# One more row group of an output projection with plain products in place of a seven-product scheme, and a new fixed order of all tasks

## The chip, the core and the metric

The kernel runs on one core of one Trainium2 chip. The metric is the device time of one execution in microseconds (us), the median over runs. The engines are named as in the profile: PE is the matrix engine (PEld its weight loads), DVE the vector engine, ACT the scalar engine, POOL the GpSimd engine, and SP the engine whose queue issues most of the transfers. Each engine works through its own instructions in the order in which the program lists them.

## The reference

Attention over 4 batches, 8 heads, 768 positions of 64 elements, followed by a gated feed-forward block over the 3072 resulting rows:

```python
scores = (q @ k^T) / 8                       # per batch and head
keep   = causal                              # heads 0, 2, 6
keep   = causal & (key < 4 | q - key < 64)   # the other heads
x      = softmax(where(keep, scores, -1e9)) @ v      # -> (3072, 512)
g      = x @ w_gate                          # (512, 1536)
out    = (g * sigmoid(g) * (x @ w_val)) @ w_out      # (1536, 512), float32
```

## The kernel before

**Tiles and groups.** Queries come in 24 tiles of 128 rows, loaded in pairs. Loads land in eleven raw buffers. A tile goes through casts (`cq`, `ck`, `cx`), transposes on PE (`trq`, `trk`) with copies out of PSUM (`evq`, `evk`), scores on PE (`sc`), exponentials on ACT (`ex`), multiplications by a 0/1 mask on DVE or POOL (`mask`, L577), value products on PE (`val`), a normalisation on DVE (`nm`), a transpose back (`xtr`) and a copy (`xe`). Four tiles make a group, so there are six groups of 512 rows. For each group, twelve column blocks of the hidden layer are made: `gate` and `vals` are four 512-column matmuls each (L732; in group 0 some are split in two halves of 256), followed by `tanh` on ACT (L738) and two DVE operations, `stt1` (L742) and `stt2` (L748), that leave the block in `h_sb`, which holds two groups at a time.

**The output projection** of a group multiplies 512 rows of hidden activations by `w_out`. It exists in two forms.

- *Plain*: for each of the four row tiles, twelve 512-column matmuls accumulate in one PSUM bank (`outproj`, L766), then one copy (`oevac`) and one 256 KB store. In terms of 2 by 2 blocks this is eight block products. Group 5 uses it.
- *Seven products*: the hidden block and `w_out` are cut into 2 by 2 blocks, and seven products of sums of blocks replace the eight (`seventh`, L812, twelve 256-column matmuls each). It needs sums of hidden blocks (`hsum`, eight per group, L799, on DVE or POOL), sums of weight blocks once for all groups (`wsum`, twelve, L412, kept in `wt_sb`), and eight gathering steps per group (`gathered`, seven additions on DVE at L828 and one copy), then two 512 KB stores. Groups 0 to 4 use it (`SEVENS = 5`).

**The order.** No scheduler decides at build time. Every step is a task of a `Plan`. Three strings, the work of an offline planner, fix everything: `ORDER` lists the tasks (and a few filler matmuls on an identity, `warm`) in the order in which they are issued, `WAYS` picks for each task which of its allowed engines runs it, and `SLOTS` picks its buffer or PSUM bank. A task issued earlier stands ahead of later ones in its engine's queue, and waits there for what it depends on.

Of the kernel before, what the change touches and what calls it, by code (L numbers as in the profile page):

```python
# [13 lines left out]


ORDER = (
    "000402061U1V071W03xx1c1d1e0920211Xy21f0C01050A22yG28292A231g1h1i1j1r1s1p1q1w081Z1b1axh2B2CzG2E2D"
    "2F2N2O2L2M2W2c2d2e0B2426252G2H2I0D2X2f1Y1k1l1m1t1u1v2g2i2h2j2l2m1n2J1o1y1z2K272P2Q2R0g0y98999A1x"
    "2t30312x382y0F3C3I3J3K0h139c9S9T9d9U0m109B9C0n140G2o2p33349e0z9I2S2U2V9D9G9h9a9E9F9H9i9j2n9V9W0E"
    "2Y2a2Z9X9Y9Z9f9g9b9J9K3D3L2b2k2q2r2s2u3M3N3O3P3U3V329k9l0i169r9m9s9t2z9n9o3R3S353637399N9O119L9M"  # L20
    "9P9Q9R0H3F3H3E3b3l3m3i3j0l1FALAGAMANAH3W3X3f0o179u9v9pAI9q3T3G0q1D3Q3Y3Z3a3g3c0k1CA6ABA7A83kA9AA"
    "ACAD2T0j3n3o0t19A19wA23h3p3q2v3r3A3B2w3d3e0r1GAJAKA3AOAP3s3t0J3v439x9y0I3u4041420p1AA4A50K3y3x3z"
    "Ax0U15AEAFATAV4446454748494H4A4BB40wAuAvAwAy9zA00P5J0M4b0u18ASB5B6BEBFBGBdBeBf0s12B7B84L4M4NB9BA"
    "BBBYBZBgBhBaBC1E1M3w0V4O4P4W4CBbBc4DAUBDAzB0B14j4k4l0RBiBjBk0x1H1Q1R1T1S4E4F4GBHBIBlBm0vB2B31B1K"
    "1I1J1LAY1N1P0L4a4g4h4i5R0N4d4f4e4cAQAXARAZAW4p4qBTBUBVBOBPBQ4m4z4R4S5S5TApAqAr0bBWBX1OAe0O5I0Y7E"
    "4n4oBJBKBL0S0e4Q5O5P5Q4I0W6X6YAcAdAfAiAj4r56574J4KAaAbAgAhAkAo4T4U4V4X53AsAt5p5v5w54554u4v4s4t5f"
    "BMBN4w5g4x4y505c5l5dBRBSBpBrBnBo5B5C595A58AlAm4Y4Z515D5E5F5xBv0T5s5t520a5q5y5z60BqBsBuByC5Bt6465"
    "0cAnBw616C625G5HC10Z7H66D5D6D7CCCDCECoD8D90Q5L5K5NClCmCnCp7mCRCSCTCgChCi5h6J6KBzC07M7N7O5rCjCk0X"
    "7D5M5e5i5j5k5mC36VC2C4C6C7CB7I6W6L5U5V5W6G6H6ID0D1D2CvCwCFCGCxCe5X5Y5ZCMCNCyCzCO7lD3D467685u7k6M"
    "6N6e6f6gCUCV6b6c6d63696A6B6DCPCQCqCrCs5a5n5b5o7q7r7s6O6P6Q6SCbCcCdCf7J7K6E6FCWCXCYBxC8C9CA7L6R6h"  # L30
    "6i6j6k6l6uCtCu6T6UCKCZCaDDDFCHCICJENEOEPCLDCDE6mEDEEEFDtDuDv7t7u7v0f8T6n6o6p6qEIEJ0d8QDADGDBDH7o"
    "7X7Y7Z7a7g7b7cDwDxEKELEMEGEH6r6s6v6tDIDLDJ8U74757172737P7Q7RDeDfDgDyDzE0EQERDZDaDb7z807G76DhDiES"
    "ETEUE1E2EVEW6aDMDN7F7d777e7f7S7T7U8RDm6y6z707w7xDcDd6w6x7i7V7W7j7pE3E4E5DODPDj6Z78797AE881DkDlDn"
    "8W8X8Y7B7CDoDpDqEB7nFBFCFD878H8I8B8CE9DQDR7yE6E7EA8E8MEC8283FLFMFNFEFFDrDs7h848588868ZFOFPFn8D8F"
    "8G8a8b8c8k8l8f8g8h8d8e8VFGFHFIFaFbFcF6F7F8FiFVFWDKF9FAFXDSEZDUEaDTEbFkFlFJFKFmDYFfFgDVDWFoFhFj8J"
    "8K8N8LEXEYEdFpFqFrFsFtFQFRFS8p91928w8xFdFe8i8j8tFTEcElEe8S8m8n8o8q8uEfEi8vF1F2EjF3En8z90EwExEhFU"
    "Es8y9394DXEkEmEgEo898r8A958s8OF49697EpEqErEtEz8PGxHCHDGnFxFzEyH2GyF5GbGzGqEvGoEuF0GpGrGiGjH0H5Gk"
    "GvH3H1H4H6GsGtGuGwFYFZGlGYGZGaGcGJGKGLFuFvFwFyG0G2G4GdGeGfGmH7H8H9GRGgGhGOGPGTHEGUG1G6G7G5GFHAG3"
    "GCHBGVGWGXGAGQGSHFHGGMGNG8G9GDGGGHHHGBGEGIHIHJHMHNHKHLHOHRHPHQHSHTHWHXHYHbHUHVHZHaHcHd"
)  # L40
WAYS = (
    "000010000000000000000000000000000000000000000000000000000000222202022222202002220010101010101212"
    "020000000000000000000000110001212222011011000000100000001000220011011000001001000001001001001000"
    "000001220111011000001001000000010000010010000000002201120000000000010000000010010010000011000200"
    "200010010010010000000210100100000000000020102000001100000001001001000010002221101000000100100000"
    "020000100100000120120000201100000000100000002200001001000000000220112000000001000000010010001101"
    "201110001001000001000001101001001000001201102020000000001000000000010010000010000000000000000000"
    "000000000000000000000000000000000000000000000000000000000000000000000000100000000100000000000000"
    "000000000000000000000000000000000000000000000000000000000000001001000100000000000000000000000000"
    "000000000000000000000000000000000000000000000000001111110011000000000000000000000000000000000000"  # L50
    "000000000000000000000000000000000000000111110000100000000000100000000000000000000000000000000000"
    "000000000000000000000000000111110100110000000000000000000000000000000000000000000000000000000000"
    "00000000000000000000000010000000000010"
)
SLOTS = (
    "0015246374927435A772A445A6315997824058A38A501609221819001016041002241222230063601254461440016340"
    "656011214224222121043652064614232261606014354644521622063602461221046162644040343654462621302145"
    "600160216141211426361623606445601310362216320614025604224614041421402642562542516163424201406465"
    "604133263222541412634461606200005010410210124411031120024500140040110012330130002110011155022233"
    "031050200011002221015001401011100100401441250120510120130251113012411115121401501220005100430000"  # L60
    "013110000200100345500000202121500000211114301100125115412010041125124052131203005501111211023311"
    "1112131134100412210200023310531201144125302011050100012411241100410131043120200002102"
)
DIGITS = "0123456789ABCDEFGHIJKLMNOPQRSTUVWXYZabcdefghijklmnopqrstuvwxyz"

# [54 lines left out]
def kernel(  # L120
# [50 lines left out]
    P = Plan(RINGS)  # L171
# [49 lines left out]
    NK, HM = NJ // 2, DM // 2  # L221
    SEVENS = 5
# [193 lines left out]
    for i in range(3):  # L416
        for x in range(1, 5):
# [3 lines left out]
                                 deps=[T_w["o", i][0], T_w["o", i + 3][0]] + before))  # L421
# [412 lines left out]
        eng.dma_start(out=out[r0:r0 + 256, :].rearrange("(s p) n -> p s n", s=2),  # L834
                      in_=out_sb[:, x])

    T_hs, T_ga, T_p, T_stored = {}, {}, {}, {}

    def tasks_of_sevens(g, T_h):
        wo = [T_w["o", j][0] for j in range(6)]  # L840
# [55 lines left out]
    for g in range(NG):  # L896
# [3 lines left out]
        for j in range(NJ):  # L900
            parts = [(0, 256), (256, 512)] if g == 0 and j < HALVES else [(0, w)]
            for c in parts:
                a = P.add(f"gate{g}.{j}.{c[0]}", ["PE"],
                          (lambda g=g, j=j, c=c: gate(g, j, c, wg_sb, gs)),
                          deps=xs[c[0] // 128:c[1] // 128] + [T_w["g", j // 2][j % 2]],
                          takes=["gv"])
                th = P.add(f"tanh{g}.{j}.{c[0]}", ["ACT"],
                           (lambda g=g, j=j, c=c: tanh(g, j, c)), deps=[a], takes=["sig"])
                s1 = P.add(f"stt1 {g}.{j}.{c[0]}", ["DVE"],
                           (lambda g=g, j=j, c=c: stt1(g, j, c)), deps=[th], takes=["sil"])  # L910
                v_ = P.add(f"vals{g}.{j}.{c[0]}", ["PE"],
                           (lambda g=g, j=j, c=c: gate(g, j, c, wv_sb, vs)),
                           deps=xs[c[0] // 128:c[1] // 128] + [T_w["v", j // 2][j % 2]],
                           takes=["gv"])
                was = [T_p[g - 2, p] for p in ((6, 7) if j < NK else (3, 4))] if g > 1 else []
                s2 = P.add(f"stt2 {g}.{j}.{c[0]}", ["DVE"],
                           (lambda g=g, j=j, c=c: stt2(g, j, c)), deps=[s1, v_] + was)
                T_h.setdefault(j, []).append(s2)
                P.uses(a, "gv", s1)
                P.uses(v_, "gv", s2)  # L920
                P.uses(th, "sig", s1)
                P.uses(s1, "sil", s2)
                P.uses(T_first_x[g], "xt", a, v_)
        if g < SEVENS:
            tasks_of_sevens(g, T_h)
            continue
        last = None
        for tt in range(SIZES[g]):
            stores = []
            for x, (ring, lo, hi) in enumerate(pieces(g, tt)):  # L930
                for third in range(3) if x == 0 else [0]:
                    js = slice(third * 4, third * 4 + 4) if x == 0 else slice(0, NJ)
                    last = P.add(
                        f"out{g}.{tt}.{3 * x + third}", ["PE"],
                        (lambda g=g, tt=tt, x=x, js=js: outproj(g, tt, x, js)),
                        deps=[y for j in range(js.start, js.stop) for y in T_h[j]]
                        + [T_w["o", j // 2][0] for j in range(js.start, js.stop, 2)],
                        takes=[] if third else [ring], after=[last])
                    if third == 0:
                        head = last  # L940
                oe = T_oe[g, tt, x] = P.add(
                    f"oe{g}.{tt}.{x}", ["ACT", "DVE"], (lambda g=g, tt=tt, x=x: oevac(g, tt, x)),
                    deps=[last] + T_stored[g - 1, tt // 2], after=stores[:1])
                P.uses(head, ring, oe)
                st = T_st[g, tt, x] = P.add(f"st{g}.{tt}.{x}", ["SP", "ACT"], (lambda g=g, tt=tt, x=x: store(g, tt, x)),
                           deps=[oe])
                stores.append(st)
            for y in stores:
                P.lands(y)


    for number in P.order():
# [40 lines left out]
```

## Time and profile before

| what | value |
|---|---|
| median of 3 runs | 259.12 us (258.81 to 259.85) |
| the profiled execution, its own time | 258.92 us |
| its span in the profile | 256.9 us |
| granted PE clock | 1.0 |
| PE busy | 246.9 us (96% of the span) |
| DVE busy | 195.2 us (76%) |
| ACT busy | 154.8 us (60%) |
| POOL busy | 154.7 us (60%) |
| moved by transfers | 34.98 MB |

The profiled execution's own time is 2.0 us above its span, and the median is 0.2 us above the profiled execution. Busy time on PE is a modelled figure, since matmuls overlap. The spacing of their starts, which the chain of waits shows (for instance 64 matmuls in 13.81 us), tells what they cost when nothing holds them.

### The profile page before, as it was taken

The page shows a single profiled execution, that of the slowest core. Times are in us where ns is not written, and L with a number is a line of the kernel's source. Part 1 is how long each engine was busy: PE and PEld are TensorE (multiplying, and loading weights), DVE is VectorE, ACT ScalarE, POOL GpSimd, SP SyncE. Part 2 cuts the span into 40 slices and gives each one's busy share as a digit, 9 for nine tenths or more (in the row PEclk, how much of TensorE's full clock was granted, in tenths as well). Part 3 has the DMA queues.
Part 4 walks back from the last instruction along what each step waited for, and adds up shares of the span by engine and source line. Part 5 has one row for each costly group of instructions (what it writes and reads, how often), then busy time and mean ns, then how long its engine had stood idle before and what let it go on. Part 6 is the DMA issues. An engine that isn't in the chain of part 4 may idle for free.

```text
span 256.9 us, 5969 instructions
## 1 busy us (share of the span) xinstructions
PE 246.9 (96%) x2368; PEld 153.8 (60%) x2368; DVE 195.2 (76%) x337; ACT 154.8 (60%) x245; POOL 154.7 (60%) x161
## 2 busy tenths in 40 slices
PE   7989899998989999999999999999999999999995
PEld 3667755643565868665675656665565874466643
DVE  1569799998999789699997859578487778776740
ACT  5799987486948775765787785765736242231011
POOL 6489999926990968659705998506876505084000
PEclk9999999999999999999999999999999999999999
DMA  7999999998860067802007000000021003000043
GB/s 189 348 357 344 331 356 357 376 387 271 276 186 0 0 189 225 245 4 82 3 3 243 2 3 0 3 1 4 1 94 72 3 0 144 22 0 3 0 184 143
DMA packets 32331, 34.98 MB, mean 136 GB/s; under 512 B 1456, under 2 KB 22192, under 8 KB 32304
## 3 DMA queue, kind: packets, MB, share of 16 engines
q1 hardware_dynamic: 31888, 33.82, 41.0%
q10 hardware_dynamic: 416, 0.79, 0.8%
q8 instruction: 18, 0.29, 0.5%
q14 instruction: 9, 0.07, 0.1%
HBM read 28.31 MB, written 6.29 MB: 135 GB/s over the span
## 4 chain that ended last, share of the span: by engine, by line
PE 65%; POOL 11%; DVE 9%; DMA 6%; SPq 5%; issue 3%; POOLq 0%; DVEq 0%
PE banks L732 33%; PE banks L812 16%; POOL e L577 7%; PE banks L560 4%; PE banks L766 4%; SPq L349 4%; DMA raw<-in_moe_w_val_dram 3%; PE banks L587 3%; DMA raw<-in_moe_w_out_dram 2%; DVE h_sb L748 2%; DVE wt_sb L412 2%; PE banks L466 2%; PE banks L606 1%; POOL wg_sb L208 1%; POOL wv_sb L208 1%
## 5 line engine op out<-in xcount | busy, mean ns | idle before, releaser
L732 PE MATMUL banks<-xt,wg_sb 128*128 128x512 f16 (+1 forms) x304 | 71.2, 368 | 3.1 <-DVE sil L742 1.7
L732 PE MATMUL banks<-xt,wv_sb 128*128 128x512 f16 (+1 forms) x304 | 70.8, 368 | 0.0
L569 ACT ACTIVATE e<-banks 128x1024 f16<-128x1024 f32 (+2 forms) x68 | 59.0, 912 | 16.7 <-PE banks L560 8.8
L738 ACT ACTIVATE sig<-banks 128x512 f32<-128x512 f32 (+1 forms) x76 | 42.9, 577 | 41.9 <-PE banks L732 36.3
L577 POOL TENSOR_TENSOR e<-e,m 128x640 f16<-128x640 f16 (+1 forms) x31 | 54.8, 1783 | 19.8 <-ACT e L569 19.3
L742 DVE SCALAR_TENSOR_TENSOR sil<-sig,banks 128x512 f32<-128x512 f32 (+1 forms) x76 | 49.3, 656 | 18.5 <-ACT sig L738 15.7
L748 DVE SCALAR_TENSOR_TENSOR h_sb<-sil,banks 128x512 f16<-128x512 f32 (+1 forms) x76 | 49.1, 655 | 7.8 <-PE banks L732 6.0
L732 PEld LDWEIGHTS <-wg_sb 128*128 128x128 f16 x304 | 28.0, 97 | 31.7 <-issue 4.7
L732 PEld LDWEIGHTS <-wv_sb 128*128 128x128 f16 x304 | 28.4, 98 | 27.8 <-issue 0.2
L812 PEld LDWEIGHTS <-h_sb 128*128 128x128 f16 x360 | 34.5, 98 | 7.4
L799 POOL TENSOR_TENSOR hs_sb<-h_sb 128x768 f16<-128x768 f16 x8 | 13.3, 1668 | 27.9 <-DVE h_sb L748 21.0
L828 DVE TENSOR_TENSOR out_sb<-banks,out_sb 128x512 f32<-128x512 f32 x35 | 23.3, 686 | 5.5 <-PE banks L812 4.9
L799 POOL TENSOR_TENSOR h_sb<-h_sb 128x768 f16<-128x768 f16 x13 | 21.4, 1642 | 6.2 <-PE banks L812 5.0
L560 PE MATMUL banks<-qT,kT 64*128 64x128 f16 x472 | 21.6, 218 | 0.5 <-DVE xb L595 0.3
L812 PE MATMUL banks<-wt_sb,h_sb 128*128 128x256 f16 x180 | 22.0, 273 | 0.0
L812 PE MATMUL banks<-wo_sb,h_sb 128*128 128x256 f16 x180 | 21.9, 273 | 0.0
L560 PEld LDWEIGHTS <-kT 64*128 64x128 f16 x472 | 14.6, 94 | 11.6 <-issue 10.1
L587 PEld LDWEIGHTS <-e 128*128 128x128 f16 x472 | 16.9, 97 | 2.8 <-issue 0.5
L208 POOL CAST hq<-raw 128x1024 f16<-128x1024 f32 (+1 forms) x16 | 16.1, 1014 | 4.0 <-DMA raw<-in_k_dram 2.9
L587 PE MATMUL banks<-vt,e 128*128 128x65 f16 x472 | 17.9, 193 | 0.4 <-POOL vt L208 0.4
L595 DVE TENSOR_TENSOR xb<-banks,rc 128x512 f16<-128x512 f32 x24 | 16.6, 691 | 1.0
L466 PE MATMUL banks<-ident,hq 128*128 128x128 f16 x192 | 14.6, 219 | 1.7 <-DVE h_sb L748 1.0
(58 smaller groups left out, 249.0 us busy)
## 6 DMA issues: line engine op xcount, KB each, us to landing
raw<-in_v_dram SPq DMA_DIRECT2D x12, 512.0 KB, 6.2
raw<-in_q_dram SPq DMA_DIRECT2D x22, 256.0 KB, 5.2
raw<-in_k_dram SPq DMA_DIRECT2D x22, 256.0 KB, 5.9
out_dram<-out_sb SPq DMA_DIRECT2D x9, 512.0 KB, 2.9
raw<-in_moe_w_gate_dram SPq DMA_DIRECT2D x6, 512.0 KB, 8.2
raw<-in_moe_w_val_dram SPq DMA_DIRECT2D x6, 512.0 KB, 8.4
raw<-in_moe_w_out_dram SPq DMA_DIRECT2D x6, 512.0 KB, 7.4
raw<-in_q_dram SPq DMA_DIRECT2D x1, 512.0 KB, 4.4
```

The source lines that it names most:

```text
L208: ENG[task.way].tensor_copy(out=dst, in_=src)
L560: nc.tensor.matmul(sc[:, c:c + n, :], weights, moving, start=first, stop=last)
L569: nc.scalar.activation(out=to, in_=src, func=AF.Exp, scale=scale)
L577: ENG[task().way].tensor_tensor(out=ev, in0=ev, in1=mm, op=ALU.mult)
L587: nc.tensor.matmul(avs[t][:, odd, n * 66:n * 66 + 65], ee, vv, start=(m == 0), stop=(m == len(bl) - 1))
L732: nc.tensor.matmul(ps, wsb[:, kk, j * 128:(j + 1) * 128], xt[:, kk, c[0]:c[1]], start=(kk == 0), stop=(kk == 3))
L738: nc.scalar.activation(out=sg[g, j, c], in_=gs[g, j, c], func=AF.Tanh, scale=0.5)
L742: nc.vector.scalar_tensor_tensor(out=sl[g, j, c], in0=sg.pop((g, j, c)), scalar=1.0, op0=ALU.add, in1=gs.pop((g, j, c)), op1=ALU.mult)
L748: nc.vector.scalar_tensor_tensor(out=hs[g, j][:, c[0]:c[1]], in0=sl.pop((g, j, c)), scalar=0.5, op0=ALU.mult, in1=vs.pop((g, j, c)), op1=A ...
L799: ENG[T_hs[g, x][part].way].tensor_tensor(out=to, in0=a, in1=b, op=op)
L812: nc.tensor.matmul(rooms[g, p][:, x], left[:, j, 128 * x:128 * x + 128], right[:, j], start=(j == 0), stop=(j == NK - 1))
L828: nc.vector.tensor_tensor(out=cell(*to), in0=rooms[g, p], in1=cell(*other), op=ALU.add)
```

## The change

Group 0 goes over to the plain form. Groups 1 to 4 keep seven products, group 5 stays plain. The eight block sums of group 0 and its eight gathering steps are no longer there, and the twelve weight sums are first read by group 1. The dependencies follow: `stt2` of group 2, which overwrites the buffer of group 0, now waits for the plain products of group 0, and the gathering of group 1 waits for the landing of group 0's four stores.

The three strings are replaced as a whole, so every engine's queue is in another order. Some tasks change engine.

| tasks | before | after |
|---|---|---|
| filler matmuls besides the first ten | 14 | 13 |
| masks | POOL 31, DVE 7 | POOL 23, DVE 15 |
| hidden block sums | POOL 26, DVE 14 | POOL 23, DVE 9 |
| weight block sums | POOL 5, DVE 7 | POOL 6, DVE 6 |
| weight casts | POOL 15, ACT 5 | POOL 14, ACT 3, DVE 3 |
| gathering additions | DVE 35 | DVE 28 |
| block products (12 matmuls of 256) | 35 | 28 |
| plain matmuls of 512 or less | 60 | 108 |
| stores | 15 | 17 |

```diff
 ORDER = ( ...
-    "000402061U1V071W03xx1c1d1e0920211Xy21f0C01050A22yG28292A231g1h1i1j1r1s1p1q1w081Z1b1axh2B2CzG2E2D"
...
+    "0306021U1Vxz1c000105071W1Xy01f1g1h0A221dzI1i1j1e1p1q1r1w232B2C041s0920212829zG2E2F2A0C2W2c2d2D2L"
...
-    T_hs, T_ga, T_p, T_stored = {}, {}, {}, {}
+    T_hs, T_ga, T_p, T_stored, T_plain = {}, {}, {}, {}, {}
...
-                was = [T_p[g - 2, p] for p in ((6, 7) if j < NK else (3, 4))] if g > 1 else []
+                was = [T_p[g - 2, p] for p in ((6, 7) if j < NK else (3, 4))] if g > 2 else (
+                    T_plain[0] if g == 2 else [])
...
-        if g < SEVENS:
+        if 0 < g < SEVENS:
             tasks_of_sevens(g, T_h)
             continue
...
-                    deps=[last] + T_stored[g - 1, tt // 2], after=stores[:1])
+                    deps=[last] + T_stored.get((g - 1, tt // 2), []), after=stores[:1])
...
-            for y in stores:
-                P.lands(y)
+            T_stored.setdefault((g, tt // 2), []).extend(P.lands(y) for y in stores)
+            T_plain.setdefault(g, []).append(last)
```

More of the change, by code (lines that the diff above doesn't have):

```diff
@@ L16 @@
 ORDER = (
-    "000402061U1V071W03xx1c1d1e0920211Xy21f0C01050A22yG28292A231g1h1i1j1r1s1p1q1w081Z1b1axh2B2CzG2E2D"
[L18 to L36, printed above, removed]
@@ L37 @@
-    "Es8y9394DXEkEmEgEo898r8A958s8OF49697EpEqErEtEz8PGxHCHDGnFxFzEyH2GyF5GbGzGqEvGoEuF0GpGrGiGjH0H5Gk"
-    "GvH3H1H4H6GsGtGuGwFYFZGlGYGZGaGcGJGKGLFuFvFwFyG0G2G4GdGeGfGmH7H8H9GRGgGhGOGPGTHEGUG1G6G7G5GFHAG3"
-    "GCHBGVGWGXGAGQGSHFHGGMGNG8G9GDGGGHHHGBGEGIHIHJHMHNHKHLHOHRHPHQHSHTHWHXHYHbHUHVHZHaHcHd"
+    "0306021U1Vxz1c000105071W1Xy01f1g1h0A221dzI1i1j1e1p1q1r1w232B2C041s0920212829zG2E2F2A0C2W2c2d2D2L"
+    "2M2N2O0B25242G2H272e2I0D2X2f081b1Y1Z1k1l1m1a1t1u1x1v2g2h2i2l2j2k2t2m2o2p0m101n1y1z1o303133262P2Q"
@@ new lines @@
+    "2R342J2K0h139c9d9S9e9T9U0g0y98999A9B0F3C3I3J3K2n2U2V9G9D9E9h9i322S2x2y389C9j0n149k9l9f9g9F9H0z9N"
+    "9I9O9P0E2Z2Y2q2b2r2s2u119Q9R9J9K9X9Y9Z0G3D3L9L9M0i162a9V9W9a9b0l1F2z3M3N3R3S3O3P3b3T3W3X9r9s9tAG"
+    "AHAI3f9m9n9o35363g37390o179p9q9u9v3Q0k0H3E3F3HALAMAN0q3l3m3U3V1CA6A71DA90j19A8AA3n3i3Y3Z3o3a3j3c"
+    "9w9x3h0rA1A2A31GAJAK3G2v3d3e2wAE0I0J3v9y3p0p1A3u4041423A0w3k3q3r434445ABAC1E3s3tA4A5ADAFAOAP0s3B"
+    "BdBeBgBbBfBhBTBUBVBYBZBaBc49120v46474H2TB4B5B64A0u4BApAq1B4L4M4N9zA0Ar0x1HAsAtAkAlAm4C4D0Q5M0V0K"
@@ new lines @@
+    "3y3w3x3z4O4P4W0M4bB9BAB7B8BBBEBF18BCBDBG4j4k4lBWBXAzB0B10L4a4g4h4iAuAv484E4F4GAn0t15AQ1M1OAR1I1J"
+    "1L4QB2B3Aw0N4c4d0P5J4p4q4r4m4n4z0O5I0T5s5r0W6Y4IASATAVAWAU0d0UAo4R4S565758BOBPBQ5NAXAaAYAZ4T4U4V"
+    "4X1K1N1PAbAc6W0f4J4K4u4vAd4e4o4s4t0R5R5S5TAxAy1Q1R1T4Y4Z595A53BlAe5p5O5PBJBKBL4w4x544y55AfAgAhAi"
+    "5B0S0bBn4f6a5Q5c5d5f5gBMBN5v5w5xBHBI5L5qBiBp1S6X5051525CBRBSBkBmBo5h0c6V5y5zAjBj5D5E5F8UBqBsBr60"
+    "5GBy5l6465666162638V5t5HCMCND0D1CjD3CbD2CcD4C7CPCOC8C9CQCACBCqCdCrCsCgChCiCk5eBuBvBwBxBz5K5i5j5m"
@@ new lines @@
+    "5k6C6G7mBt0Y7E7M7N7OCe0X7D6H6ICHCICJ6M6NCf5U5V0eC0C2C16ZClCmCn6J6K6R676b6c6dCKCLCU5W5X5Y685ZCvCw"
+    "Cx7J7K5a5n5b5o696A6D6BCyCzCRCSCTCV6L0a7k7q7r6e6f6g5u6O6P6QCWCXCY6SCtCuCZ6T6U0Z7G7I7LCaD87p6k6l6m"
+    "7sC3C4C56E6F6h6u6i6j7P7Q7RCoCpDUDVDWENEOEPEQER6n6o6p6q7oCCCDCE7lEDEEEF7n6r6s6t6v74757172738QDXDY"
+    "EIEJEKDc7X7Y7Z7a7g7b7cC6CFCGD7D9DoDpDqDZDaDrDsDbDdD5D6DBELEMDADC7HEGEH7t7u7vE8E9EADtDuDv8283DDDG"
+    "DEDFEBEC7F7S7d7e7f7T7U7z8081DHDI6y6z7076777wDJDK6w7i6x7V7W7j787x7y798W8X8YDh7ADeDfDgDiDLDM7h8485"
@@ new lines @@
+    "8886878B8CE17B7CDyDzE0E2E6E3E4E5E78R8Z8a8E8F8G8H8I8DDjDkDlDQFGFHFIDNEUDODRDPDSDT8M8c8d8eFaFbDwDx"
+    "FcDmDnEVEXFLFMFNFJFKFOFPFBFCFDF1F2F3F4F5FVFWFXF6F78k8l8b8f8g8hF9FEFFF8FAEwExEy8J8K8N8LFfFgEWFkFl"
+    "FdFeFhFYFZFm8p91928w8x8yESETEYFnFo8T8i8j8t8zEaEbEcEk8S8m8u8v8n8q908oErEsEtEZEuEvFiFjFQFRFS939489"
+    "8r958O8P8AEzFTFUEeEfEi9697EgEhEjEmElEdEnEoEp8sGsGxGyGdGeGbGzGvGEGtGuGwGiGqEqGfGHGjGFFsFuF0GGFpFq"
+    "GIGnGoGlGMFwGkGmGTGWFrGpGYGUGZGrGVGXH5GOGJGKGaFxGcG0GRGLG7FyHAGPGNGQGSH7H8H9HBH0H1G5H2H3H4H6GgGh"
@@ L40 @@
+    "FtG3FvFzG1G2G4G8GAGBGCG6G9GDHCHDHEHFHGHHHIHJHKHLHMHNHOHPHRHSHQHTHWHUHVHXHY"
 )
 WAYS = (
[L42 to L50, printed above, removed]
@@ L51 @@
-    "000000000000000000000000000000000000000111110000100000000000100000000000000000000000000000000000"
-    "000000000000000000000000000111110100110000000000000000000000000000000000000000000000000000000000"
-    "00000000000000000000000010000000000010"
+    "000001000000000000000000000000000000000000000000000000000000221222222201012222200110111000101112"
+    "220101100000000000000000210022022222011001000000000000000100222220001000000001000000200000000000"
+    "002201220201000000001000000000010010010010000000002001100100010010010000022000010000000010002202"
@@ new lines @@
+    "100100000000000000000120000000100000000020001000000000100000001001000210122221201100000100100000"
+    "220100100100000220002011100000000100100000001201000001000000001200200000001001000000000000002100"
+    "221111001001000001000002101000001000002100120002010000000001000000021010000010000000000000000000"
+    "000000000000000000000000000000000000000000000000000000000000000000000000010000010001000010000000"
+    "000000000000000000000000000000000000000000000000000000001110100011000000000000000000000000000000"
@@ L54 @@
+    "000000000000000000000000000000000000000000000011101001100000000000000000000000000000000000000000"
+    "000000000000000000000000000000000100011000110000000000000000000000000000000000000000000000000000"
+    "000000000000000000000001011110011000000000000100000000000000000000000000000000000000000000000000"
+    "000000000000001000000000100000011"
 )
 SLOTS = (
-    "0015246374927435A772A445A6315997824058A38A501609221819001016041002241222230063601254461440016340"
-    "656011214224222121043652064614232261606014354644521622063602461221046162644040343654462621302145"
@@ L58 @@
[L58 to L62, printed above, removed]
+    "00173254620398382967413402A936127A845A9415681740A63572001016041004122621321063201446561240102340"
@@ new lines @@
+    "616231652244204120240632421214654162606214310236460611025216060010324362406562143446165610423220"
+    "624140226020114216320611246265624231360616442600042204563601041043615612242414212221646211406345"
+    "614200262446561603424321606223021312211240003211300010004002141000121001111230121212510124000130"
+    "151100014210100034121002541242100101501011025102401015501010010540140022011540133101211401021020"
+    "001311023201343012011042011010500020121210030113001101211201012212410210042115500310131110101430"
@@ L63 @@
+    "0021010103012200251100523254021144015311030142110410030142111300110203111301210210"
 )
```

## The prediction

> **What bounds the kernel now.** I read the profile in four steps: busy shares, stretches of ten microseconds, the chain of waits, and the timeline where the chain leaves PE. The stretches come first. (Columns: window, PE with its instruction count, PEld, DVE, ACT, POOL, granted clock, transfer share, GB/s.)
>
> ```profile
> 20.00:30.00 10.00, 9.45 (x133) 7.96 (x132) 8.08 (x20) 9.33 (x18) 9.41 (x13) 1.00 1.12 335
> 30.00:40.00 10.00, 9.64 (x120) 5.78 (x117) 9.49 (x21) 8.90 (x15) 9.87 (x10) 1.00 1.09 356
> 40.00:50.00 10.00, 9.71 (x104) 5.61 (x103) 9.40 (x19) 6.01 (x9) 9.94 (x10) 1.00 1.09 363
> 50.00:60.00 10.00, 8.78 (x69) 4.52 (x68) 9.67 (x16) 6.52 (x10) 4.80 (x5) 1.00 1.00 357
> 70.00:80.00 10.00, 8.41 (x74) 5.12 (x73) 9.76 (x17) 5.80 (x10) 6.53 (x7) 1.00 0.45 136
> 210.00:220.00 10.00, 10.00 (x57) 5.28 (x56) 6.75 (x11) 2.87 (x6) 3.28 (x2) 1.00 0.28 107
> ```
>
> From 30 to 60 us DVE is full, POOL is full until 50, and PE has holes; late in the run PE alone is full. The chain says the same (start, length, what):
>
> ```profile
> 36.76 3.44 POOL e L577 x2
> ...
> 47.25 6.11 DMA raw<-in_moe_w_out_dram
> ...
> 55.48 0.57 DVE hs_sb L799
> 56.07 0.56 DVE h_sb L799
> 56.63 1.81 DVE e L577
> ...
> 70.24 1.28 DVE wt_sb L412
> 71.54 1.26 DVE wt_sb L412
> ...
> 82.25 1.31 PE banks L812 x12
> ...
> 211.83 13.81 PE banks L732 x64
> ```
>
> Between 23 and 79 us the chain runs through POOL and DVE, and much of it is work for group 0's seven products: block sums (L799) and weight sums (L412). Afterwards it is nearly all PE, except around 172 to 188 us. The last lines give PE's price when nothing holds it: 0.216 us for 512 columns (13.81 / 64), 0.109 us for 256 (1.31 / 12).
>
> PE's instructions at such prices: gates and values 544 x 0.216 + 64 x 0.108 = 124.4; block products 420 x 0.109 = 45.8; group 5's plain matmuls 10.4; score matmuls 472 x 0.034 and value products 472 x 0.030, both from their runs in the chain, 30.2; transposes 16.0; fillers 5.2; mask matmuls 2.7. Sum 234.6 us. PE runs from 1.4 to 253.9 us, so it loses 17.8 us, 2 of it in the slow first matmuls. Counting along PE's timeline, the sum reaches 10, 30, 40, 60 and 80 us at 14.7, 40.0, 50.1, 74.3 and 95.7 us. So the loss is 5.3 us between 10 and 30, 0.1 up to 40, 4.2 up to 60, 1.4 up to 80, and 3.6 in all the rest.
>
> **The change part by part.**
>
> *Group 0's products.* Seven products, 84 x 0.109 = 9.2 us, go; 48 plain matmuls, 48 x 0.216 = 10.4 us, come. PE +1.2, and one filler less: +1.0 us, on the path, as PE is full from 80 us on. Nothing hides it.
>
> *Group 0's sums and gathering.* Gone from DVE: six block sums (0.55 to 1.09, together 3.9 us) and seven additions at 0.686 (4.8 us); from POOL two sums (3.3 us). New are three copies on DVE at 0.684 and one on ACT at 0.588. Taken alone, DVE gets 6.6 us lighter and POOL 3.3.
>
> *The replanned order spends this.* Eight masks move from POOL to DVE, three weight casts come to DVE, block sums move to POOL. With every task at the mean of its row and engine, DVE totals 207.3 us before and after, and POOL falls from 157 to 140. So the question is where the DVE work stands. I counted it between the same marks of PE's sum (before and after, scaled by 195.2 / 207.3 because neighbouring DVE instructions overlap, and likewise for the others):
>
> | PE's sum | before took | DVE | ACT | POOL |
> |---|---|---|---|---|
> | 10 to 30 | 25.3 | 21.7, then 24.6 | 22.8, then 22.3 | 22.5, then 21.4 |
> | 30 to 40 | 10.1 | 9.7, then 8.6 | 5.4, then 9.0 | 10.1, then 7.6 |
> | 40 to 60 | 24.2 | 23.5, then 17.6 | 16.4, then 16.5 | 18.3, then 11.2 |
> | 60 to 80 | 21.4 | 17.2, then 21.1 | 17.8, then 15.2 | 14.4, then 15.4 |
> | 80 to end | 158.2 | 117.6, then 118.4 | 82.1, then 84.2 | 81.8, then 74.6 |
>
> - 40 to 60: DVE filled 23.5 of 24.2 us, which is why PE lost 4.2. In it stood three block sums of group 0 (1.7 us), five weight sums (4.5 us) and a mask (1.9 us). All leave this stretch, and no engine is asked for more than 17.6 us beside PE's 20. I take a loss of 1.0 in place of 4.2: -3.2 us (bounds -4.2, and 0 if something else held PE).
> - 10 to 30: DVE is asked for 24.6 us, 2.9 more, since four masks and a cast now stand there. It idled 3.6 us in that stretch, but partly for want of input. I take +1.0 (bounds 0 and +2.9).
> - 60 to 80: DVE 21.1 beside 20 of PE (three copies, six weight sums and four masks). Late here are the `stt2` results for group 1's first product. +0.5 (bounds -1.4 and +2).
> - 80 to the end: DVE is equal, POOL lighter by 7. Counting PE's work between a PE step and the one that needs its result through one to three other tasks, and taking off those tasks' durations, about 33 steps before have under 0.5 us left, after it about 20; in the last 35 us nine before and none after. I take 2.6 lost in place of 3.6: -1.0 (bounds -3.6 and +3).
>
> *Masks on DVE, and a rule against them.* The timeline has one mask of 128x1024 in 0.68 us and another, started while POOL worked on a mask, in 1.89:
>
> ```profile
> 56.48 1.41 POOL L577 TENSOR_TENSOR e<-e,m 128x640 f16<-128x640 f16 x1 [5.14 <-ACT e L569]
> 56.55 1.89 DVE L577 TENSOR_TENSOR e<-e,m 128x1024 f16<-128x1024 f16 x1
> ...
> 173.03 0.68 DVE L577 TENSOR_TENSOR e<-e,m 128x1024 f16<-128x1024 f16 x1
> ```
>
> The Trainium skill, "SBUF — State Buffer", section "SBUF: two separate sides", says that DVE and POOL share one port pair as an exclusive lock: a DVE operation with two SBUF inputs that meets a POOL operation waits until that one is over. The pair above fits. The mean of the row (1.2) already has such waits in it; that is what I use. By the rule at its worst each early mask costs 1.9 where I counted 1.2 (1.0 for the two smaller ones), so the four of the stretch 10 to 30 add 3 us to the 24.6, and the sum would be some 2 us higher. With fewer POOL instructions the rule also has fewer meetings to act on, so I keep the mean, and the worst goes to a rival.
>
> *Loads, stores, queues.* SP's queue keeps the loads; up to a PE sum of 80 they are 24 MB after and 23 before. The last w_out load is the 37th of SP's loads in place of the 38th. Group 0's stores are four of 256 KB, one issued on ACT's queue between copies and exponentials. An issue took SP about 0.6 us; ACT has 60% load, which covers it. On the path it would be 0.6 us. Group 1's gathering waits for these stores; about 3 us to land, with some 10 us of PE work between. Group 2's `stt2` now waits for the end of group 0's products, which lie a whole group back; uncovered, it would hold DVE and everything queued behind it. The end is the same plain group 5, with its last two stores on two queues in place of one: 0 to -0.1.
>
> Sum: +1.0 - 3.2 + 1.0 + 0.5 - 1.0 = -1.7 us from 258.9 gives 257.2; the median of the runs lies 0.2 above the profiled execution, so **257.4 us**.
>
> **The rivals.** About 0.5% (1.3 us) is what a measurement of this kernel can tell from no change, so faster means below 257.8 and slower above 260.4.
>
> - *The loads are the bound up to 60, not DVE.* For: the transfer share is 1.00 to 1.12 from 10 to 60 us, and a w_out load of 6.11 us lies on the chain. Against: PE's two waits in that part, 1.2 and 1.0 us, end on DVE, and 70 to 80 has DVE at 9.76 with transfers at 0.45. Then only the +1.0 on PE stays, and perhaps +0.5 at 60 to 80: 260.1 to 260.6.
> - *DVE becomes the bound earlier (the slower side).* Four masks before PE's sum reaches 30, each held by POOL for its full length: 24.6 + 3 = 27.6 us of DVE where the stretch took 25.3 and DVE has to wait for its first inputs. It decides once DVE's added work (5.9) passes its idle time there (3.6): +2.3 and up, and the backlog eats most of the gain from 40 to 60. 259.1 + 1.0 + 2.3 + 0.5 - 1.0: about 261.9. For: DVE at 9.5 from 30 us on. Against: POOL too is asked for less there, and of the trace's seven DVE masks three took 0.7, two 1.2 to 1.3, and only one 1.9.
> - *The order does more:* the holes at 40 to 60 and most of those after 80 close. 259.1 + 1.0 - 4.2 - 2.4 + 1.0: 254.5.
> - That the change does not do what it says is excluded by the code: group 0 has no block sum left in it.
>
> **How the numbers follow.** The main case has 0.55 (its own range 255.4 to 259.0; 0.44 below 257.8, 0.11 above). Loads 0.17 (0.09 same, 0.08 slower). DVE early 0.20 (0.02 same, 0.18 slower). More 0.08, faster. Faster 0.52, same 0.22, slower 0.26. The range 254.6 to 261.8 leaves out half of the last case and half of the early-DVE one.
>
> **What would show it.** Right: 48 more 512-column matmuls at L766 and 84 fewer at L812; the chain leaves POOL and DVE for PE before 70 us instead of 79; PE's sum reaches 60 by about 72 to 73 us, with DVE clearly under 9 in the stretches from 50 to 70; the mean of the DVE masks stays near 1.2. Wrong: first gate matmul later than 22 us or PE's sum of 30 later than 42, with DVE masks near 1.9 (early DVE); the same holes at 40 to 60 with loads ending the waits (loads); or new waits of PE on DVE or POOL after 80 us that sum to over 5 us.

## The result and the profile after

The changed kernel takes 256.79 us (median of 5 runs, 256.56 to 257.74) against 259.08 us before: a ratio of 0.9915, with a 95% interval of 0.989 to 0.9939. It is faster by 2.3 us. Forecast were 257.4 us and "faster" as the likeliest.

The profiled execution of the changed kernel took 257.74 us, the longest of the five, with a span of 256.0 us and a mean granted clock of 0.993. A second profiled execution of the same kernel (run `after_again`) took 256.25 us with a span of 254.5 us at clock 1.0. Both are used below. The stretches of the first (window, PE with its instruction count, PEld, DVE, ACT, POOL, granted clock, transfer share, GB/s):

```profile
20.00:30.00 10.00, 9.04 (x109) 7.54 (x104) 7.61 (x21) 7.93 (x13) 9.67 (x12) 0.83 1.10 347
30.00:40.00 10.00, 10.00 (x124) 6.80 (x122) 8.06 (x20) 9.23 (x19) 7.96 (x10) 1.00 1.11 346
40.00:50.00 10.00, 10.00 (x125) 6.07 (x124) 9.57 (x17) 8.99 (x15) 9.48 (x9) 1.00 1.07 373
50.00:60.00 10.00, 10.00 (x77) 4.96 (x73) 8.10 (x14) 5.84 (x12) 0.46 (x1) 1.00 1.11 347
...
70.00:80.00 10.00, 9.82 (x91) 5.02 (x89) 8.31 (x15) 6.79 (x11) 7.50 (x10) 1.00 0.01 3
```

From 30 us on PE has hardly a hole. DVE, at 9.67 from 50 to 60 and 9.76 from 70 to 80 before, is at 8.10 and 8.31. The transfer share is as high as it was up to 60 us. The granted clock of 0.83 in the first row is new.

The chain of waits of the same execution (start, length, what) now runs on PE from 28 us on. It leaves it between 58 and 79 us, for w_out's casts and the weight sums, where PE still had other work, and comes back with the first plain products:

```profile
38.47 2.59 PE banks L732 x12
...
51.80 6.06 PE banks L732 x28
...
70.52 2.27 POOL wt_sb L412 x2
...
80.36 1.73 PE banks L766 x8
...
90.07 2.59 PE banks L766 x12
...
242.51 10.40 PE banks L766 x60
```

A plain matmul takes 2.59 / 12 = 0.216 us, as counted, and the page has 84 + 24 of them at L766 and 336 block matmuls at L812.

PE's sum (its instructions at their own price) gives the same table as in the forecast. "Loss" is the time that a stretch took beyond PE's own work.

| kernel, time of its profiled execution | 10 reached at | loss 10 to 30 | 30 to 40 | 40 to 60 | 60 to 80 | 80 to end | PE's whole work |
|---|---|---|---|---|---|---|---|
| before, 258.92 | 14.7 | 5.3 | 0.1 | 4.2 | 1.4 | 3.5 | 234.6 |
| after, 257.74 | 15.0 | 6.0 | -0.5 | 1.2 | 1.7 | 3.9 | 235.6 |
| after_again, 256.25 | 14.2 | 5.3 | -0.5 | 1.2 | 1.7 | 3.9 | 235.6 |

(A price is a mean, so a loss can come out slightly below zero.) PE loses 3.0 us less between 40 and 60, and pays 1.0 us more work and 0.4 more loss later.

How before's losses split at the mark of 60 is not firm. PE's sum passes 60 just ahead of a hole of 1.0 us that ends at 74.3, so it matters on which side of the hole the mark is set: counted matmul by matmul, the stretches 40 to 60 and 60 to 80 lose 2.0 and 3.6 us in place of 4.2 and 1.4. Their sum is 5.6 either way, against 2.9 after (2.7 by the other count).

### The profile page after: what moved, and what is told of

It reads as the page before. It is cut to its first block, busy times and chain, and to the rows that moved or that the text cites. A ratio compares the mean times of both kernels' runs of the same rounds, so it can differ in the third digit from the quotient of the medians.

```text
span 256.0 us, 5874 instructions
## 1 busy us (share of the span) xinstructions
PE 248.0 (97%) x2331; PEld 151.9 (59%) x2331; DVE 189.4 (74%) x330; ACT 154.5 (60%) x256; POOL 138.5 (54%) x145
## 4 chain that ended last, share of the span: by engine, by line
PE 85%; DVE 6%; POOL 4%; issue 2%; DMA 1%; ACT 1%; POOLq 0%; DVEq 0%
PE banks L732 44%; PE banks L812 15%; PE banks L560 7%; PE banks L766 6%; PE banks L587 5%; PE banks L466 4%; PE banks L321 3%; PE banks L606 2%; POOL wt_sb L412 1%; DMA raw<-in_q_dram 1%; DVE xb L595 1%; DVE vt L212 1%; POOL e L577 1%; DVE sil L742 1%; POOL hq L208 1%
## 5 line engine op out<-in xcount | busy, mean ns | idle before, releaser
L569 ACT ACTIVATE e<-banks 128x1024 f16<-128x1024 f32 (+2 forms) x68 | 59.7, 911 | 18.1 <-PE banks L560 13.3
L577 POOL TENSOR_TENSOR e<-e,m 128x640 f16<-128x640 f16 (+1 forms) x23 | 39.7, 1737 | 29.4 <-ACT e L569 13.7
L799 POOL TENSOR_TENSOR h_sb<-h_sb 128x768 f16<-128x768 f16 x14 | 22.8, 1640 | 35.3 <-DVE hs_sb L799 24.6
L812 PEld LDWEIGHTS <-h_sb 128*128 128x128 f16 x288 | 27.5, 98 | 5.9 <-DVE h_sb L748 0.2
L828 DVE TENSOR_TENSOR out_sb<-banks,out_sb 128x512 f32<-128x512 f32 x28 | 18.9, 689 | 5.1 <-PE banks L812 4.4
L208 POOL CAST hq<-raw 128x1024 f16<-128x1024 f32 (+1 forms) x19 | 17.9, 951 | 7.8 <-DMA raw<-in_q_dram 4.7
L766 PE MATMUL banks<-wo_sb,h_sb 128*128 128x512 f16 (+2 forms) x108 | 21.7, 355 | 0.0
L587 PEld LDWEIGHTS <-e 128*128 128x128 f16 x472 | 17.3, 98 | 4.1 <-DVE vt L212 1.2
L587 PE MATMUL banks<-vt,e 128*128 128x65 f16 x472 | 18.6, 195 | 1.1 <-DVE vt L212 1.1
L812 PE MATMUL banks<-wo_sb,h_sb 128*128 128x256 f16 x144 | 17.7, 273 | 0.0
L812 PE MATMUL banks<-wt_sb,h_sb 128*128 128x256 f16 x144 | 17.2, 273 | 0.0
L766 PEld LDWEIGHTS <-h_sb 128*128 128x128 f16 x108 | 9.9, 98 | 10.1
## 6 DMA issues: line engine op xcount, KB each, us to landing
raw<-in_k_dram SPq DMA_DIRECT2D x22, 256.0 KB, 6.0
raw<-in_q_dram SPq DMA_DIRECT2D x22, 256.0 KB, 4.9
out_dram<-out_sb SPq DMA_DIRECT2D x4, 256.0 KB, 2.8
```

The costliest lines, as they stand in the source:

```text
L208: ENG[task.way].tensor_copy(out=dst, in_=src)
L569: nc.scalar.activation(out=to, in_=src, func=AF.Exp, scale=scale)
L577: ENG[task().way].tensor_tensor(out=ev, in0=ev, in1=mm, op=ALU.mult)
L587: nc.tensor.matmul(avs[t][:, odd, n * 66:n * 66 + 65], ee, vv, start=(m == 0), stop=(m == len(bl) - 1))
L766: nc.tensor.matmul(o_open[g, tt, x], hs[g, j][:, tt * 128:(tt + 1) * 128], wo_sb[:, j, lo:hi], start=(j == 0), stop=(j == NJ - 1))
L799: ENG[T_hs[g, x][part].way].tensor_tensor(out=to, in0=a, in1=b, op=op)
```

## The experiments

Two kernels are made from the kernel before to ask what held PE in the stretch 40 to 60 (each leaves out part of the work), five to ask which part of the change gives the gain; one run repeats the kernel after, and four kernels vary it. Each group shared a chip with fresh runs of the kernel before (258.95 to 259.04 us).

**Group 0's sums made thin, `before_thin_sums`.**

```diff
-            out=wt_sb[:, x - 1, ks], in0=a[:, ks], in1=b[:, ks], op=ALU.subtract)
+            out=wt_sb[:, x - 1, ks, 0:16], in0=a[:, ks, 0:16], in1=b[:, ks, 0:16], op=ALU.subtract)
...
+        n = 16 if g == 0 else 256      # hsum: columns summed
```

> The kernel before with the twelve weight sums and group 0's eight block sums on 16 of 256 columns only (the rest of the sums is left out, and two DVE memsets at the start stand in), so that all waits remain and about 5 us of DVE and 7 us of POOL work go. Relief theory: PE's loss between 40 and 60 falls from 4.2 to about 1: 256 to 257 us. Loads theory: 259, within 0.5.

Measured: 255.17 us, ratio 0.9845 (0.9818 to 0.9873). The loss between 40 and 60 falls from 4.2 to 1.7 us, and between 60 and 80 from 1.4 to 0.1. So the work of the sums, and not the waits that come with them, held PE; the gain of 3.9 us is larger than expected, because it also ran on past 60. (The edit takes work from POOL as well as from DVE, so it does not tell the two apart; the change moves or drops only part of this work.) DVE itself hardly empties between 50 and 60 us: it goes from 9.67 to 9.25, and yet PE's holes are gone.

```profile
50.00:60.00 10.00, 10.00 (x79) 5.10 (x79) 9.25 (x19) 6.70 (x11) 4.88 (x6) 1.00 1.00 362
```

So it is not the share of DVE's time that PE feels, but when single DVE results come.

**Half of w_out's loads, `before_half_wout`.**

```diff
-                out=r.rearrange("p (a n) -> p a n", a=2), in_=wod[:, 2 * n:2 * n + 2, :])
+                out=r[:, 0:512], in_=wod[:, 2 * n, :])
```

> The kernel before with half of each w_out block loaded (the other half of the weights is taken from the same rows), so 1.6 MB less to load before 60 us, over 4 us of transfer time; the casts and all else stay. Relief theory: 259, within 0.7, as DVE and POOL still fill the stretch. Loads theory: PE's loss between 40 and 60 falls by 2 to 4 us: 255 to 257 us.

Measured: 258.93 us, ratio 1.0 (0.9982 to 1.0018). Its stretches beside those of the kernel before:

```profile
40.00:50.00 10.00, 9.70 (x104) 5.58 (x103) 9.39 (x19) 6.04 (x9) 9.94 (x10) 1.00 1.08 363
50.00:60.00 10.00, 8.78 (x69) 4.52 (x68) 9.67 (x16) 6.49 (x10) 4.77 (x5) 1.00 0.55 190
```

From 50 to 60 us the transfer share falls from 1.00 to 0.55, and PE stays at 8.78 and DVE at 9.67, to the last digit. The loads were not what PE waited for there, although a w_out load of 6.11 us lay on the chain. The loads theory falls for this stretch. (Up to 50 us the transfer share is unchanged, so whether loads hold PE earlier is not tested.)

**Plain products in the old order, `structure_only`, `plain_old_order`.** These keep the order of before. The three thirds of each plain row tile stand at the places of the products p2, p1, p7 and p5, each copy follows a few tasks later, and block sums and gathering of group 0 go. In structure_only the fourth store leaves only after group 1's gathering has written to its buffer; plain_old_order sends it earlier. In task names, shortened:

```diff
-  ... hs0.* oe0.* out0.p1 ... out0.p7 st0.h0 st0.h1
+  at out0.p2: out0.0.*   at out0.p1: out0.1.*   at out0.p7: out0.2.*   at out0.p5: out0.3.*
+  at st0.h1: the stores of group 0
```

> The order of before is kept; only group 0's products become plain, at the places of the seven, and its block sums and gathering go. The weight sums stay where they were. Relief theory (group 0's sums filled DVE while PE's sum went from 40 to 60): DVE there falls from 23.5 to 21.7 us, PE's loss from 4.2 to about 2, PE's work rises by 1.2: 258 to 258.7 us, and PE's sum of 60 comes at 72 to 73 instead of 74.3. Loads theory (transfers bind up to 60 us): 260.2. Whole-order theory (the gain is the replanned order's alone): 260 or more.

> As structure_only, with all four stores of group 0 issued ahead of group 1's first gather (in structure_only the fourth store left after that gather had written to its buffer). All theories: the stores hold nothing, 259.0 within 0.4, with PE's sum of 60 near 72 us and the gain given back after 80.

Measured: 258.99 us (ratio 0.9997, 0.9984 to 1.001) and 258.90 us (0.9994, 0.9984 to 1.0004). None of the theories has this total: it lies above the 258 to 258.7 of the relief theory and below the 260 of the others. Placed like this in the old order, the plain form is worth nothing. It does what it should and gives it back:

| kernel | loss 40 to 60 | 60 to 80 | 80 to end | PE's whole work |
|---|---|---|---|---|
| before | 4.2 | 1.4 | 3.5 | 234.6 |
| plain_old_order | 1.2 | 1.1 | 5.9 | 235.8 |
| after_again | 1.2 | 1.7 | 3.9 | 235.6 |

In the kernel before, PE has three holes of over 0.5 us between 50 and 80 us, 2.8 us together (1.22, 0.99 and 0.60), and each ends on DVE. plain_old_order has none. The timeline shows how the first comes about (engine, line, operation, tiles, count). First the kernel before, then plain_old_order:

```profile
56.07 0.56 DVE L799 TENSOR_TENSOR h_sb<-h_sb 128x768 f16<-128x768 f16 x1
...
56.48 1.41 POOL L577 TENSOR_TENSOR e<-e,m 128x640 f16<-128x640 f16 x1 [5.14 <-ACT e L569]
56.55 1.89 DVE L577 TENSOR_TENSOR e<-e,m 128x1024 f16<-128x1024 f16 x1
...
58.73 0.69 DVE L742 SCALAR_TENSOR_TENSOR sil<-sig,banks 128x512 f32<-128x512 f32 x1
...
59.47 1.02 PE L732 MATMUL banks<-xt,wg_sb 128*128 128x512 f16 x4 [1.22 <-DVE sil L742]
```

```profile
55.56 0.69 DVE L577 TENSOR_TENSOR e<-e,m 128x1024 f16<-128x1024 f16 x1
...
56.52 1.41 POOL L577 TENSOR_TENSOR e<-e,m 128x640 f16<-128x640 f16 x1 [5.14 <-ACT e L569]
...
57.27 0.69 DVE L742 SCALAR_TENSOR_TENSOR sil<-sig,banks 128x512 f32<-128x512 f32 x1 [0.76 <-ACT sig L738]
57.30 1.89 PE L732 MATMUL banks<-xt,wg_sb 128*128 128x512 f16 x8
```

Two block sums stood ahead of the mask in DVE's queue. They took 1.1 us themselves, and pushed the mask from 55.6 to 56.55, into POOL's mask, where it took 1.89 us in place of 0.69. `stt1` came 1.5 us late, the PSUM bank was freed late, and PE idled 1.22 us. With the sums gone DVE is through before POOL starts.

The second hole is another matter. First the kernel before:

```profile
70.16 2.65 DVE L412 TENSOR_TENSOR wt_sb<-wo_sb,wt_sb 128x512 f16<-128x512 f16 x2
...
71.82 1.47 PE L812 MATMUL banks<-wo_sb,h_sb 128*128 128x256 f16 x12
...
73.56 1.87 DVE L748 SCALAR_TENSOR_TENSOR h_sb<-sil,banks 128x512 f16<-128x512 f32 x3
74.29 1.21 PE L466 MATMUL banks<-ident,hq 128*128 128x128 f16 x16 [0.99 <-DVE h_sb L748]
```

Then plain_old_order:

```profile
68.86 2.17 DVE L412 TENSOR_TENSOR wt_sb<-wo_sb,wt_sb 128x512 f16<-128x512 f16 x2
...
70.53 2.75 PE L766 MATMUL banks<-wo_sb,h_sb 128*128 128x512 f16 x12
...
71.79 1.87 DVE L748 SCALAR_TENSOR_TENSOR h_sb<-sil,banks 128x512 f16<-128x512 f32 x3
...
73.12 1.06 PE L466 MATMUL banks<-ident,hq 128*128 128x128 f16 x16
```

Two weight sums stand ahead of `stt2` in DVE's queue in both. In plain_old_order they take 0.5 us less, and PE works on twelve matmuls of 512 columns in place of twelve of 256 (1.3 us more) while it would have waited. So part of PE's added work went into a hole.

After 80 us plain_old_order has holes that the kernel before does not have:

```profile
89.31 0.82 PE L587 MATMUL banks<-vt,e 128*128 128x65 f16 x22 [0.85 <-ACT e L569]
...
99.13 0.48 DVE L577 TENSOR_TENSOR e<-e,m 128x640 f16<-128x640 f16 x1
...
99.66 0.72 PE L587 MATMUL banks<-vt,e 128*128 128x65 f16 x18 [0.97 <-DVE e L577]
```

The value products of tiles 9 and 11 wait for an exponential and a mask. In the kernel before, a block product stood between the scores and each of these and covered that wait, the first of them here:

```profile
87.99 1.47 PE L812 MATMUL banks<-wt_sb,h_sb 128*128 128x256 f16 x12
...
89.30 0.83 PE L587 MATMUL banks<-vt,e 128*128 128x65 f16 x22
```

I left the places of p6, p4 and p3 empty, and both new holes lie at such places. So the loss after 80 belongs to this placing; whether another placing in the old order keeps the gain was not run. In all 2.4 us more are lost after 80 than before, and 1.2 us of PE work are added: 3.0 + 0.3 - 2.4 - 1.2 leaves about nothing.

**The weight sums in a block, `structure_late_sums`.** As structure_only (its fourth store leaves in the same late place), with the twelve weight sums moved behind group 0's last copy.

> As structure_only, and the twelve weight sums are issued only after group 0's last copy, as group 1 is their first reader. Relief theory: DVE between PE's sums of 40 and 60 falls to 18.1 us, POOL to 12; PE's loss there to about 1: 257 to 257.8 us. Loads theory: 260.2, as structure_only. Whole-order theory: 260 or more, or a new wait of group 1's products on the late sums.

Measured: 266.78 us, ratio 1.0288 (1.0261 to 1.0315), 8 us slower than structure_only. The relief theory's 257 to 257.8 missed. Most of it is a new wait of 5.9 us (timeline), and the granted clock, 0.985 to 0.987 in all four executions, adds to it:

```profile
89.23 2.66 DVE L412 TENSOR_TENSOR wt_sb<-wo_sb,wt_sb 128x512 f16<-128x512 f16 x2 [0.72 <-POOL wt_sb L412]
...
91.81 1.37 DVE L412 TENSOR_TENSOR wt_sb<-wo_sb 128x512 f16<-128x512 f16 x1
...
93.21 3.87 DVE L412 TENSOR_TENSOR wt_sb<-wo_sb,wt_sb 128x512 f16<-128x512 f16 x4
...
97.24 0.69 DVE L595 TENSOR_TENSOR xb<-banks,rc 128x512 f16<-128x512 f32 x1
...
97.98 1.01 PE L560 MATMUL banks<-qT,kT 64*128 64x128 f16 x14 [5.90 <-DVE xb L595]
```

Seven sums in a row are 7.9 us of DVE, the normalisation of a tile stands behind them, and the scores wait 5.9 us for its PSUM bank. That the first reader of the sums comes later does not make it safe to put them together; the new order spreads them from 69 to 94 us (in after_again), six on each of the two engines, with other work between.

**The early masks, both ways.** `masks_old_order` is the kernel before with the masks mask4.0, mask5.0, mask5.1 and mask6.1 on DVE in place of POOL; `plain_and_masks` is plain_old_order with the same; `early_masks_pool` is the kernel after with the same four back on POOL.

In task names:

```diff
 WAYS: tasks mask4.0 mask5.0 mask5.1 mask6.1
-  POOL
+  DVE          (early_masks_pool: from DVE to POOL)
```

> The kernel before, order and all, with only the four early masks (tiles 4 to 6) taken from POOL to DVE. POOL theory (POOL's fill was what held PE between sums of 10 and 50, in before too): PE's sum of 30 comes 1 to 2 us earlier and 257 to 258 us. Both-full theory (DVE is as full as POOL there as long as group 0's sums stand in its queue): same within 0.7, or slower by up to 2.

> plain_old_order with the four early masks on DVE as well: both parts of the change in the old order. If the two parts make the gain, 256.5 to 257.5; if the new order of everything else is needed (the waits after a PE sum of 80 that plain_old_order met), 258.5 or more.

> The kernel after with the four early masks (tiles 4 to 6, before PE's sum of 30) back on POOL, as before had them. Early-DVE theory (these masks made the stretch 10 to 30 longer): 10 to 30 shortens by about 0.7, 256.0. POOL theory (POOL is the fuller engine from 20 to 50 us, and 7 us of masks there hold PE): 1 to 3 us slower, 258 to 260.

| kernel | us | ratio to before | loss 10 to 30 | 30 to 40 | 40 to 60 | 80 to end |
|---|---|---|---|---|---|---|
| masks_old_order | 263.27 | 1.0179 (1.0142 to 1.0216) | 8.7 | 1.4 | 2.7 | 4.6 |
| plain_and_masks | 264.95 | 1.023 (1.0205 to 1.0255) | 9.6 | 1.4 | 1.1 | 5.5 |
| early_masks_pool | 260.92 | 1.0063 (1.0041 to 1.0084) | 9.0 | 0.3 | 1.2 | 3.9 |
| after_again | 256.57 | 0.9901 (0.9878 to 0.9924) | 5.3 | -0.5 | 1.2 | 3.9 |

The same four masks cost 4.3 us when they are moved to DVE in the old order, and 4.3 us when they are moved to POOL in the new one. For the old order both theories missed (plain_and_masks did come out above 258.5, but with the same mask holes and not for the reason forecast); for the new one the POOL theory held in sign and was too small. Neither engine is right by itself. In the new order with the masks on POOL, POOL is full and DVE half empty:

```profile
20.00:30.00 10.00, 7.47 (x81) 6.02 (x81) 4.94 (x13) 5.32 (x10) 9.59 (x10) 0.83 1.10 348
30.00:40.00 10.00, 10.00 (x134) 7.25 (x133) 6.17 (x16) 9.20 (x19) 9.67 (x12) 1.00 1.11 345
```

PE then waits for POOL's other tasks, casts and copies that stand behind the masks (who waited for whom: us in total, times, longest):

```profile
PE banks L587 <- POOL vt L208: 1.7, 1, 1.7
PE banks L732 <- POOL wg_sb L208: 0.8, 2, 0.5
```

The half-clock spell in the first row (0.83) is not the cause of the loss: the one execution at clock 1.0 took 260.72 us, and the others 260.73 to 261.21.

In the old order a mask on DVE stands behind what the list has ahead of it. In before, POOL did mask4.0 at 27.18. With mask4.0 on DVE (timeline of masks_old_order):

```profile
30.80 0.41 DVE L742 SCALAR_TENSOR_TENSOR sil<-sig,banks 128x256 f32<-128x256 f32 x1
31.23 0.68 DVE L212 TENSOR_REDUCE vt<-raw 64x512 f16<-64x512 f32 x1
...
31.94 0.69 DVE L577 TENSOR_TENSOR e<-e,m 128x1024 f16<-128x1024 f16 x1
```

It starts at 31.94, behind `stt1`, `stt2` and value casts, and tile 4's value products leave a hole of 2.8 us on PE. In its waits PE's value products stand 3.7 us for DVE's masks, which the kernel before does not have:

```profile
PE banks L587 <- DVE e L577: 3.7, 2, 2.8
```

**The half-clock spell, `after_again`, `early_fill`, `less_fill`.** In the first profile of after, PE ran at half its clock for 3.41 us from 20.7 us on (not from 20.2, as an expectation below has it):

```profile
22.00:23.00 1.00, 1.00 (x20) 0.80 (x16) 1.00 (x3) 0.77 (x2) 1.00 (x2) 0.50 1.15 325
23.00:24.00 1.00, 1.00 (x19) 1.00 (x17) 0.43 (x2) 1.00 (x2) 0.90 (x2) 0.50 1.19 299
24.00:25.00 1.00, 1.00 (x11) 0.87 (x10) 0.96 (x3) 0.52 (x2) 1.00 (x2) 0.93 1.09 354
```

Two of the five executions had a mean clock of 0.993 and took 257.6 and 257.74; the three at 1.0 took 256.56 to 256.79. So a spell costs about 1 us in this kernel. I tried filler matmuls in PE's holes, and fewer of them. In task names:

```diff
 ORDER, early_fill                       ORDER, less_fill
+  four fillers behind val0.0            -  the two fillers ahead of sc2.0
+  two fillers behind sc4.1
```

> The kernel after once more, to stand beside the next three on one chip. All theories: 256.8, with some executions about 1 us longer and at a mean clock of 0.993, the others at 1.0.

> The kernel after with six filler matmuls in two holes of PE: four behind val0.0 (a hole of 1.2 us) and two behind sc4.1 (0.5 us). Clock theory (PE's half-rate spell of 3.4 us, seen from 20.2 us on in the profile of after, follows from PE's holes between 15 and 20 us): every execution at clock 1.0, all at 256.5 to 256.8, PE's sum of 30 about 1 us earlier than in a run with the spell. Rival (the spell has another cause): spells as often as without, or fillers that delay the early work by up to 1.3 us.

> The kernel after without the two filler matmuls ahead of sc2.0 (0.43 us of PE work at 12.5 us). Clock theory: spells in most executions or a longer one, 257.5 to 258.5. Rival (another cause, or fillers only cost): 256.4 to 256.8, spells no more often.

Measured: 256.57 us (six executions, 256.25 to 257.68, one at 0.993), 256.58 (six, 256.44 to 257.1, none below 0.999) and 256.31 (four, 256.25 to 256.35, none below 0.998; ratio 0.9884, 0.9863 to 0.9904). Taking fillers away did not bring spells in these four, which the clock theory wanted; adding six cost nothing and gained nothing, and no spell in six cannot be told from the three in eleven executions of the kernel after. What goes with large holes is clearer: early_masks_pool, with a hole of 1.7 us that ends at 23.1 us, had 0.993 or less in three of four executions, masks_old_order and plain_and_masks, with 2.8 us, 0.994 or less in seven of eight, and structure_late_sums, with its 5.9 us, 0.985 to 0.987 in all four. What decides between a spell and none at holes of 0.4 to 1.1 us stays open. less_fill is the fastest of the kernels that leave nothing out, but its interval overlaps that of after_again.

**One more mask to DVE, `less_fill_mask`.** less_fill with the second mask of tile 4 on DVE.

> less_fill (after without two fillers) with one more early mask, that of tile 4's second unit (1.4 us on POOL at 23.7 us), on DVE. POOL theory: POOL is still at 9.7 of 10 from 20 to 30 us, PE's loss between sums of 10 and 30 falls by 0.3 to 1 us: 255.4 to 256. Rival (that stretch is bound by the loads' and PE's own chains by now): 256.3, within 0.3.

Measured: 257.19 us, ratio 0.994 (0.9916 to 0.9964), slower than less_fill by 0.9, so both theories missed. The loss between 10 and 30 rose from 4.5 to 4.9. It lacks the same two fillers as less_fill, and two of its five executions had a clock of 0.993. This one mask is better left on POOL; no other single task was tried.

## Why the prediction was right, point by point

- *PE's added work, +1.0:* as counted. The two profiles differ by 1.0 us in PE's sum.
- *40 to 60, -3.2, and 60 to 80, +0.5:* measured -3.0 and +0.3, and the sum of the two, -2.7, is the firm figure. DVE's queue held PE and the loads did not, which the thin sums, the halved loads and the three holes that end on DVE show. The working was too broad, though: it credited five weight sums that leave the stretch, of which the trace has only two on DVE ahead of 74.3 us. plain_old_order keeps the weight sums where they were and loses as little as after. The first hole came from two block sums in front of one mask and that mask's meeting with POOL; the second closed in plain_old_order with the weight sums still ahead of `stt2`, in part because PE had longer work there. "Nothing hides it" was therefore too strong for the added PE work.
- *10 to 30, +1.0:* measured 0.0 at full clock, +0.7 in the execution with the spell. One mis-sized term is the DVE mask. I took the old row's 1.2 us; after has

```profile
L577 DVE TENSOR_TENSOR e<-e,m 128x1024 f16<-128x1024 f16 x10 | 7.6, 764 | 3.6 <-ACT e L569 3.5
```

  (by form: busy time and mean duration, then idle time) 0.76 us for the large and 0.59 for the small ones. (Of before's seven masks on DVE the working lists six; the seventh took 1.62 us.) DVE was busy for 20.1 us of the stretch (14.2 to 39.5 us in after_again), where 24.6 were counted; the four masks account for 2.0 of the difference, with 2.4 us in place of 4.4, and the rest is not explained. The rule of the Trainium skill, "SBUF — State Buffer", "SBUF: two separate sides", was right in kind: a mask that waits for POOL's to end at 57.89 and then takes 0.69 would have taken 2.03 us from 56.55 on, and took 1.89. But the number of meetings belongs to an order and does not carry over to another. The rival of an early DVE bound fell with it: DVE is at 7.61 and 8.06 from 20 to 40 us.
- *Masks as a mere burden* was the deeper slip. In the forecast the masks on DVE only cost. early_masks_pool shows that in the new order they save 4.3 us, as PE would wait for casts and copies on a full POOL. I had the row: POOL at 9.41 to 9.94 from 20 to 50 us.
- *After 80, -1.0:* +0.4. Counting steps with little distance on PE from what they need (33 before, 20 after) did not foretell this; the losses there were small already. Against plain_old_order, whose placing leaves gaps, the new order loses 3.9 in place of 5.9.
- *30 to 40* gained 0.6 and the start 0.5 (in after_again), which were not forecast. The start varies between executions, see below.

The sum: -0.5 + 0.0 - 0.6 - 3.0 + 0.3 + 0.4 + 1.0 = -2.4, which is the difference of the two spans at full clock, 254.5 and 256.9.

The total is right in part by luck. The term of 10 to 30 was too high by 1.0 us and that of 80 to the end too low by 1.4, and 1.1 us of gain at the start and from 30 to 40 were not forecast. Two of the signs did not come either: the chain is back on PE at 79 us and not before 70, and the mean of the large DVE masks is 0.76 us and not near 1.2.

So the theory that group 0's sums in DVE's queue held PE holds for the stretch. For the total, the plain form frees about 3 us; the new order keeps most of them, and the one placing tried in the old order did not. Which part of the new order does it, beyond the early masks, is not shown.

## What to carry to other kernels

When work leaves a full engine, look up what stands next in every queue where PE will now arrive early; in a fixed order the freed time can be given back at a step whose wait was covered by work that is now gone. Which engine a task is best on depends on its place in that engine's list, so a changed assignment wants a new order, and a new order wants its own look at which operations meet on DVE and POOL. Count an engine's load by stretches, but find the instructions whose lateness PE sees before crediting the whole load: with DVE still busy for 9.25 of 10 us, PE had no hole left.

## What was not expected of the hardware

PE's clock moved from execution to execution of the same program. Between 5 and 6 us PE worked on three filler matmuls in one profile of after and on five in the other, and PE's sum of 10 came at 15.0 and 14.2 us. (The rows give a granted clock of 1.00 there in both, so the spacing alone tells it: 0.43 us from one filler to the next at first, 0.22 later.) The half-clock spell of 3.41 us in the middle of a busy stretch cost about 1 us; in the 3.41 us before it PE was busy for 1.92 us by the trace (17.3 to 20.7 us), so no idle stretch of that length came first. A DVE mask that was through before POOL's began took 0.69 us at the place where one that started 0.07 us behind it took 1.89.
